# A constant's tile made 128 bytes wider in a three-stage Fourier and MoE kernel

## The chip, the cores and the metric

The kernel runs on one core of a Trainium2 chip. The metric is the device time of one launch in microseconds (us), from the inputs in HBM to the output in HBM. Lower is better.

## What is computed

Three layers follow each other on 6016 rows (2 sequences of 3008) of 256 numbers, all in float32:

```python
X = np.fft.rfft(x, axis=1)
Yr = Xr @ w_r - Xi @ w_i + b_r
Yi = Xr @ w_i + Xi @ w_r + b_i
Yr, Yi = soft_shrink(Yr, 0.01), soft_shrink(Yi, 0.01)
x = np.fft.irfft(Yr + 1j * Yi, n=3008, axis=1).reshape(6016, 256)
h = x @ w_in                                   # 256 -> 2048
x = (h * np.clip(h + 3.0, 0.0, 6.0) / 6.0) @ w_out
g = x @ w_gate                                 # 256 -> 1536
out = (g / (1 + np.exp(-g)) * (x @ w_val)) @ w_out2
```

(`soft_shrink` stands for two lines of the reference.) The weights come as float64 and are turned into pairs of float32 numbers in the kernel.

## The kernel before

**Stages.** The transform comes first, as small products with tables (`pre`, L275; `s2`, L336; `ln`, L356 to L375; `ia`, L382). `post` (L473) finishes the way back for one block of tokens. The first expert layer runs in units: 12 blocks of 512 or 448 tokens times 16 slices of 128 hidden columns. A unit is `project1` (six matmuls into `ph`, L117 to L119) and, two units later, `outp` (six into `acc`). The second expert layer runs in 72 quads: 6 pairs of token blocks times 12 hidden slices. A quad has seven products of three matmuls each (`product`, L716 to L718, into the banks `P`, `Tb`, `Q`) and, for the quad before it, four shares of three (`share`, again L117 to L119, into `acc`). Here the two token blocks of a pair enter through sums and differences that are held in seven tiles `xo`, the moving operands of the products.

**Three matmuls for a product.** Every operand of the expert layers and of `ln` is held as a high and a low part of type float32r, and each product is low times high, high times low, high times high (`mm3`, L116). In a matmul the first operand is the stationary one, which is loaded into the array ahead of it, and the second moves through. The other products (`pre`, `s2`, `ia`, `post`) take float32 operands, and the trace shows two matmul records for each.

**Order of work.** The schedule is manual: each engine runs its instructions in the order in which the program issues them, and the order is written out in `seq`, `unit` and `quad`. DMAs go out on SP's queue, a few on those of ACT and POOL. Nothing in the order depends on an address.

**Where tiles lie.** SBUF is filled from two ends. Pools of the side "left" are stacked from low addresses up, those of the side "right" from high addresses down. The left side begins with a scratch area of 8192 bytes and four constants of 32 bytes each; then come `misc` (L124), `wst` (L134), `rings` (L207) and later `cv` (L566). The right side holds `edge` (L136, 480 bytes that nothing uses), `w1`, for the transform `attn`, and from the second layer on `p2` (L696). The seven tiles `xo` of pair p are taken from the pool `xo[p % 2]` (L646): pairs 0, 2 and 4 from `cv` on the left, pairs 1, 3 and 5 from `p2` on the right (L624, L697). The addresses in the built program, in bytes within a partition:

| tiles | side | first byte | remainder by 512 |
|---|---|---|---|
| `fwd1_sb`, `inv2_sb`, `three` | left | 8320, 9088, 9472 | 128, 384, 256 |
| `zeros` and all tiles of `wst`, `rings` (`room0`, `room1`, `xa`, `r`, `ct`, `gh`, `gl`) | left | 9600 to 66944 | 384 |
| tiles of `cv`: `full`, `slot`, `raw`, `xo` of pairs 0, 2, 4, `T` | left | 68992 to 155008 | 384 |
| tiles of `attn` (`linh`, `linl`, `X`, `room2`, `room3`, `z`, `m`, `n`, `yp`) | right | 70144 to 161280 | 0 |
| `w1`, the weights of the first layer | right | 163328, 196096 | 0 |
| tiles of `p2`: `c`, `h`, `s`, `xo` of pairs 1, 3, 5 | right | 181760 to 224768 | 0 |

The 128-column slices of the weights that one matmul loads are 512 bytes long, and the rows of all operands in the expert layers are multiples of 512 bytes apart, so a slice has the remainder of its tile. In `ln` the slices of `X` have the remainders 0 and 256, and `linh`, `linl` 0.

Of the kernel before, what the change touches and what calls it, by code (L numbers as in the profile page):

```python
# [9 lines left out]
F32 = mybir.dt.float32  # L10
# [71 lines left out]
def fourier_moe_kernel(ctx: ExitStack, tc: tile.TileContext, x, lin, bias, w1, w2, fwd1, inv2, fwd2,  # L82
# [3 lines left out]
    def pool(stack, name, side):  # L86
        return stack.enter_context(tc.tile_pool(name=name, bufs=1, side=side))
# [36 lines left out]
    misc = pool(ctx, "misc", "left")  # L124
    fwd1_sb = misc.tile([128, 2 * GW], F32, name="fwd1_sb")
    inv2_sb = misc.tile([GW, QP], F32, name="inv2_sb")

    three = misc.tile([128, 32], F32, name="three")[:, :1]
    nc.vector.memset(three, 3.0)
    zeros = misc.tile([128, 512], F32, name="zeros")  # L130
    nc.vector.memset(zeros, 0.0)
# [731 lines left out]
```

## Time and profile before

| | us |
|---|---|
| median of 3 runs | 1259.88 (1257.68 to 1259.9) |
| the profiled execution's own time | 1258.6 |
| its span, first to last instruction | 1256.8 |
| TensorE (PE) busy | 1240.8 |
| VectorE (DVE) busy | 811.7 |
| ScalarE (ACT) busy | 679.9 |

The span is what the trace covers; the time of the execution is 1.8 us longer. PE's clock was granted at 0.998 of full speed on the mean. Matmuls are pipelined and the trace models their ends, so the busy time of PE says only that it hardly ever stood still; how fast it went is read from the starts of its matmuls or from the mean length of one.

### The profile page before, as it was taken

How to read it: one execution, taken by the hardware profiler on the slowest of the kernel's cores; microseconds unless marked ns; L12 is line 12 of the kernel's file. 1: busy time of each engine (PE TensorE's matmuls, PEld its weight loads, DVE VectorE, ACT ScalarE, POOL GpSimd, SP SyncE). 2: the span in 40 equal slices, each digit the busy share in tenths (PEclk: the TensorE clock that was granted, in tenths of full speed). 3: DMA queues.
4: the chain of work that ended last, by engine and by line, in shares of the span. 5: the costliest groups of instructions: out<-in, count | busy, mean ns of one | idle time of the engine just before them, and what ended most of it. 6: DMA issues, size and time to landing. Idle time of an engine off the chain costs nothing.

```text
span 1256.8 us, 15921 instructions
## 1 busy us (share of the span) xinstructions
PE 1240.8 (99%) x5914; PEld 1033.7 (82%) x5914; DVE 811.7 (65%) x1426; ACT 679.9 (54%) x1216; POOL 11.1 (1%) x19
## 2 busy tenths in 40 slices
PE   8899999999999999999999999999999999999998
PEld 3799887888888888888899888888888888888897
DVE  3577685666666666566556577676676666666665
ACT  3355554555555555555455566555656555555554
POOL 3000000000000000000000000000000000000000
PEclk9999999999999999999999999999999999999999
DMA  7886233023132122132032244544644644544551
GB/s 276 301 260 203 72 93 106 26 99 102 63 99 94 55 79 76 63 99 90 38 105 90 75 177 171 201 170 151 218 156 172 230 151 151 214 154 163 207 184 73
DMA packets 48781, 172.90 MB, mean 138 GB/s; under 512 B 4720, under 2 KB 18256, under 8 KB 37072
## 3 DMA queue, kind: packets, MB, share of 16 engines
q1 hardware_dynamic: 41600, 162.85, 37.6%
q10 hardware_dynamic: 6912, 8.39, 1.9%
q8 instruction: 46, 0.75, 0.2%
q0 software_dynamic: 192, 0.66, 0.1%
q14 instruction: 31, 0.25, 0.1%
HBM read 132.81 MB, written 39.06 MB: 137 GB/s over the span
## 4 chain that ended last, share of the span: by engine, by line
PE 97%; DMA 2%; DVE 1%; ACT 1%; issue 0%; SPq 0%; ACTq 0%; DVEq 0%
PE acc L118 12%; PE acc L119 12%; PE acc L117 12%; PE ph L117 7%; PE ph L119 7%; PE ph L118 7%; PE P L716 5%; PE P L718 5%; PE P L717 5%; PE Tb L718 3%; PE Tb L717 3%; PE Tb L716 3%; PE p L473 3%; PE p L117 2%; PE p L119 2%; PE p L118 2%
## 5 line engine op out<-in xcount | busy, mean ns | idle before, releaser
L488 DVE SCALAR_TENSOR_TENSOR r<-r,ph 128x512 f32<-128x512 f32 (+1 forms) x192 | 129.5, 675 | 91.1 <-ACT r L487 91.0
L487 ACT ACTIVATE r<-ph,three 128x512 f32<-128x512 f32 (+1 forms) x192 | 130.2, 678 | 103.7 <-PE ph L119 88.4
L122 DVE TENSOR_TENSOR gl<-r,gh 128x512 fp32r<-128x512 f32 (+1 forms) x192 | 130.0, 677 | 81.0 <-ACT gh L506 79.7
L506 ACT CAST gh<-r 128x512 fp32r<-128x512 f32 (+1 forms) x192 | 117.4, 611 | 83.9 <-DVE r L488 81.4
L117 PE MATMUL ph<-xa,w 128*128 128x512 f32 (+1 forms) x384 | 153.4, 400 | 0.0
L117 PE MATMUL acc<-gh,w 128*128 128x512 f32 (+1 forms) x384 | 149.8, 390 | 1.0 <-ACT gh L506 1.0
L118 PE MATMUL acc<-gl,w 128*128 128x512 f32 (+1 forms) x384 | 149.9, 390 | 0.3 <-DVE gl L122 0.2
L119 PE MATMUL ph<-xa,w 128*128 128x512 f32 (+1 forms) x384 | 149.8, 390 | 0.0
L118 PE MATMUL ph<-xa,w 128*128 128x512 f32 (+1 forms) x384 | 149.7, 390 | 0.0
L119 PE MATMUL acc<-gh,w 128*128 128x512 f32 (+1 forms) x384 | 149.7, 390 | 0.0
L122 DVE TENSOR_TENSOR gl<-s,gh 128x512 fp32r<-128x512 f32 (+1 forms) x144 | 97.2, 675 | 49.7 <-ACT gh L740 49.7
L716 PE MATMUL P<-xo,slot 128*128 128x512 f32 (+1 forms) x288 | 111.8, 388 | 1.7 <-DVE g L786 0.8
L118 PE MATMUL acc<-gl,slot 128*128 128x512 f32 (+1 forms) x288 | 111.9, 388 | 0.3 <-DVE gl L122 0.2
L718 PE MATMUL P<-xo,slot 128*128 128x512 f32 (+1 forms) x288 | 111.4, 387 | 0.0
L119 PE MATMUL acc<-gh,slot 128*128 128x512 f32 (+1 forms) x288 | 111.4, 387 | 0.0
L717 PE MATMUL P<-xo,slot 128*128 128x512 f32 (+1 forms) x288 | 111.4, 387 | 0.0
L117 PE MATMUL acc<-gh,slot 128*128 128x512 f32 (+1 forms) x288 | 111.1, 386 | 0.0
L782 ACT ACTIVATE s<-g 128x512 f32<-128x512 f32 (+1 forms) x72 | 44.9, 623 | 94.2 <-DVE g L780 94.2
L740 ACT CAST gh<-s 128x512 fp32r<-128x512 f32 (+1 forms) x144 | 88.2, 612 | 1.5 <-DVE s L799 1.2
L117 PEld LDWEIGHTS acc<-gh,w 128*128 128x128 f32 x384 | 72.3, 188 | 16.6 <-ACT gh L506 1.4
L118 PEld LDWEIGHTS acc<-gl,w 128*128 128x128 f32 x384 | 72.3, 188 | 16.1 <-DVE gl L122 1.0
L119 PEld LDWEIGHTS acc<-gh,w 128*128 128x128 f32 x384 | 72.3, 188 | 15.1
(102 smaller groups left out, 2263.3 us busy)
## 6 DMA issues: line engine op xcount, KB each, us to landing
slot<-Wd SPq DMA_DIRECT2D x72, 1152.0 KB, 5.1
st<-in_w SPq DMA_DIRECT2D x68, 256.0 KB, 3.6
Wd<-slot SPq DMA_DIRECT2D x12, 1152.0 KB, 4.7
z<-Bd SPq DMA_DIRECT2D x12, 512.0 KB, 5.6
Cd<-cs ACTq DMA_DIRECT2D x12, 512.0 KB, 3.6
Xd<-x SPq DMA_DIRECT2D x20, 256.0 KB, 2.1
raw<-Xd SPq DMA_DIRECT2D x5, 1024.0 KB, 7.6
out_t<-osb SPq DMA_DIRECT2D x20, 256.0 KB, 2.2
```

Of the source, the lines that this page charges most:

```text
L117: nc.tensor.matmul(o, wl, xh, start=start, stop=False)
L118: nc.tensor.matmul(o, wh, xl, start=False, stop=False)
L119: nc.tensor.matmul(o, wh, xh, start=False, stop=stop)
L122: nc.vector.tensor_tensor(out=o, in0=full, in1=hi.bitcast(F32), op=ALU.subtract)
L487: nc.scalar.activation(r[:, :n], p[:, :n], AF.Relu, bias=three)
L488: nc.vector.scalar_tensor_tensor(out=r[:, :n], in0=r[:, :n], scalar=6.0, in1=p[:, :n], op0=ALU.min, op1=ALU.mult)
L506: nc.scalar.copy(hi[:, :n], g[:, :n])
L716: nc.tensor.matmul(o, wl, x[:, 0, :n], start=start, stop=False, skip_group_check=not start)
L717: nc.tensor.matmul(o, wh, x[:, 1, :n], start=False, stop=False, skip_group_check=not start)
L718: nc.tensor.matmul(o, wh, x[:, 0, :n], start=False, stop=True, skip_group_check=not start)
L740: nc.scalar.copy(hi[:, :nb], t[:, :nb])
L782: nc.scalar.activation(s0[:, :n], h, AF.Silu)
```

## The change

`three` is a tile of 128 bytes of which one float is used. It becomes 256 bytes wide. No instruction is added, removed or moved.

```diff
@@ -125,7 +125,7 @@
     fwd1_sb = misc.tile([128, 2 * GW], F32, name="fwd1_sb")
     inv2_sb = misc.tile([GW, QP], F32, name="inv2_sb")
 
-    three = misc.tile([128, 32], F32, name="three")[:, :1]
+    three = misc.tile([128, 64], F32, name="three")[:, :1]
     nc.vector.memset(three, 3.0)
     zeros = misc.tile([128, 512], F32, name="zeros")
     nc.vector.memset(zeros, 0.0)
```

Every left tile behind `three` begins 128 bytes higher, so at a multiple of 512 bytes. `fwd1_sb`, `inv2_sb`, `three` itself and all tiles of the right side stay where they are.

## Rows read from the trace of the kernel before

**Rows 1.** The page: busy time of each engine, and the chain that ended last.
```profile
PE 1240.8 (99%) x5914; PEld 1033.7 (82%) x5914; DVE 811.7 (65%) x1426; ACT 679.9 (54%) x1216; POOL 11.1 (1%) x19
...
PE 97%; DMA 2%; DVE 1%; ACT 1%; issue 0%; SPq 0%; ACTq 0%; DVEq 0%
```

**Rows 2.** Groups by shape, whole span: count, busy us, mean ns of one.
```profile
L119 PE MATMUL ph<-xa,w 128*128 128x512 f32 x320 | 126.3, 395 | 0.0
...
L119 PE MATMUL acc<-gh,w 128*128 128x448 f32 x64 | 23.4, 366 | 0.0
...
L716 PE MATMUL P<-xo,slot 128*128 128x512 f32 x240 | 94.2, 392 | 1.5 <-DVE g L786 0.8 <-ACT x L496 0.8
```

**Rows 3.** Five windows of 60 us in pairs 0 to 4: PE busy, (x) matmuls.
```profile
730.00:790.00 60.00, 60.00 (x266) 1.00 0.45 159
810.00:870.00 60.00, 60.00 (x260) 1.00 0.51 182
900.00:960.00 60.00, 60.00 (x267) 1.00 0.54 195
1000.00:1060.00 60.00, 60.00 (x260) 1.00 0.44 159
1090.00:1150.00 60.00, 60.00 (x267) 1.00 0.48 172
```

**Rows 4.** Groups by shape, PE, window 730 to 790 us (pair 0).
```profile
L717 PE MATMUL P<-xo,slot 128*128 128x512 f32 x33 | 12.8, 389 | 0.0
...
L117 PE MATMUL acc<-gh,slot 128*128 128x512 f32 x32 | 12.4, 389 | 0.0
```

**Rows 5.** The same for the window 810 to 870 us (pair 1).
```profile
L718 PE MATMUL P<-xo,slot 128*128 128x512 f32 x32 | 12.6, 394 | 0.0
L117 PE MATMUL acc<-gh,slot 128*128 128x512 f32 x32 | 12.5, 391 | 0.0
...
L717 PE MATMUL Q<-xo,slot 128*128 128x512 f32 x8 | 3.2, 397 | 0.0
```

**Rows 6.** Timeline of PE in pair 0: start us, length us.
```profile
744.69 0.39 PE L717 MATMUL P<-xo,slot 128*128 128x512 f32 x1
...
746.96 0.39 PE L718 MATMUL P<-xo,slot 128*128 128x512 f32 x1
```

**Rows 7.** Timeline of PE in pair 1.
```profile
846.33 0.39 PE L717 MATMUL Tb<-xo,slot 128*128 128x512 f32 x1
...
848.88 0.39 PE L117 MATMUL acc<-gh,slot 128*128 128x512 f32 x1
```

**Rows 8.** Groups by shape, PE, window 426 to 462 us (first layer).
```profile
L118 PE MATMUL ph<-xa,w 128*128 128x512 f32 x27 | 10.7, 395 | 0.0
...
L118 PE MATMUL acc<-gl,w 128*128 128x512 f32 x26 | 10.3, 394 | 0.0
```

**Rows 9.** The tile `linh` (stage `ln`): lengths in ns min/median/max.
```profile
L119 PE MATMUL p<-linh,X x192: 279/283/288, 33.5 to 193.3; 128*128 128x256 f32 x192
```

**Rows 10.** Groups by shape, PE, window 1180 to 1240 us (pair 5).
```profile
L118 PE MATMUL acc<-gl,slot 128*128 128x448 f32 x36 | 13.2, 368 | 0.0
L716 PE MATMUL P<-xo,slot 128*128 128x448 f32 x36 | 13.2, 365 | 0.0
...
L117 PE MATMUL acc<-gh,slot 128*128 128x448 f32 x36 | 13.0, 362 | 0.0
```

**Rows 11.** Groups by shape, PE, windows 10 to 13.3, then 13.4 to 16.7 us.
```profile
L275 PE MATMUL p<-room,fwd_sb 128*96 128x512 f32 x9 | 4.0, 592 | 0.0
```

**Rows 12.** Groups by line, PE, whole span: `post`.
```profile
L473 PE MATMUL p<-inv_sb,ct 96*128 96x94 f32 (+14 forms) x300 | 35.6, 269 | 0.0
```

**Rows 13.** Windows over all engines: PE, PEld, DVE, ACT busy us.
```profile
430.00:460.00 30.00, 30.00 (x131) 24.33 (x130) 18.52 (x36) 15.94 (x27) 0.00 (x0) 1.00 0.33 104
820.00:850.00 30.00, 30.00 (x130) 24.23 (x130) 21.53 (x34) 17.01 (x30) 0.00 (x0) 1.00 0.44 158
```

**Rows 14.** What PE waited for: us in total, times, longest us.
```profile
PE p L275 <- DMA room<-in_x: 4.7, 1, 4.7
...
PE acc L117 <- ACT gh L506: 1.0, 1, 1.0
```

**Rows 15.** The tile `room`: time of its loads from issue to landing.
```profile
DMA to landing us min/median/max: 4.7/6.3/8.0
```

## The prediction

> **What bounds the kernel now.** I read the page first. PE is busy for 99% of the span, and the chain that ended last lies 97% on PE [rows 1]. So a change that touches no instruction can only matter through the rate of the matmuls or through the few waits of PE. I then split the matmuls by shape [rows 2], and compared stretches that do the same work.
>
> The second expert layer gives that comparison. Its pairs 0 to 4 run the same quads with the same engines beside them. Yet in 60 us PE starts 266 or 267 matmuls in pairs 0, 2 and 4, and 260 in pairs 1 and 3, all with the clock at 1.00 (2.4 GHz) and PE never idle [rows 3]. By shape, every one of the twelve groups of pair 0 has a mean of 389 ns [rows 4]; in pair 1 the groups lie between 391 and 397 [rows 5], 393.8 weighted by their counts. The ends are modelled, so I checked the starts: ten steps in pair 0 take 2.27 us, 227 ns each [rows 6]; eleven in pair 1 take 2.55 us, 232 ns each [rows 7]. A difference in mean length is a difference in spacing.
>
> What alternates with the pairs is the place of `xo`: left in 0, 2, 4, right in 1, 3, 5. The stationary `slot` and the moving `gh`, `gl` are on the left in all. With `slot` and `xo` both at remainder 384 the spacing is 227 ns; with `slot` at 384 and `xo` at 0 it is 232. The shares of pair 1, whose own operands both lie at 384, are slow too (391 for L117), so an unequal neighbour disturbs them: the weights of one matmul are loaded while another one streams.
>
> The first layer fits. Its weights are at 0, its moving `xa`, `gh`, `gl` at 384, and its groups have 394 or 395 ns [rows 8], as in the odd pairs. And `ln`, with 256 columns, has both operands on the right, at 0 or 256 against 0: its median is 283, and no matmul of the 192 in the row is longer than 288 [rows 9]. My reading: a float32r matmul goes at 389 ns (512 columns) where the stationary and moving operands begin at the same place modulo 256 bytes, and 5 to 6 ns slower where they are 128 bytes apart.
>
> **The change part by part.** It lifts the left side by 128 bytes: remainder 384 becomes 0, which is that of the right side. Under the reading all float32r matmuls then meet equal remainders.
>
> First layer, 512 columns: 6 groups of 320 = 1920 matmuls [rows 2]. In a stretch without `post` the six groups average 394.8 [rows 8], against 389: 5.8 ns x 1920 = 11.2 us.
>
> First layer, 448 columns: 6 x 64 = 384 matmuls at 366 [rows 2]. No row shows them at the fast spacing. I take the straight line between the two fast rows, 283 at 256 columns and 389 at 512 [rows 4, 9]: 0.414 ns a column, so 389 - 64 x 0.414 = 362.5. That gives 3.5 x 384 = 1.3 us.
>
> Pairs 1 and 3: 12 quads x (21 + 12) = 396 matmuls each, 792 at 393.8 against 389: 4.8 x 792 = 3.8 us.
>
> Pair 5, mostly 448 columns: 396 matmuls; its twelve groups lie between 362 and 370, 365.4 weighted, of which three stand here [rows 10]. 365.4 - 362.5 = 2.9, x 396 = 1.1 us.
>
> Pairs 0, 2 and 4 and `ln`: already equal, 0.
>
> Sum: 11.2 + 1.3 + 3.8 + 1.1 = 17.4 us.
>
> Against it stand the operands that do not move. `inv2_sb` stays at 384 while `ct` goes to 0, so `post` turns from equal to unequal; in `pre`, `fwd1_sb` stays while `room0` and `room1` move. These are float32. The `pre` row has 592 ns in the window of `room1` (384, weights at 0) and the identical 592 in that of `room2` (0, weights at 0) [rows 11]. I take 0, and as the far end 5.8 ns on each of the 300 matmuls of `post` [rows 12], 1.7 us.
>
> What hides the rest: PE faster by 2.4% asks the same of DVE and ACT. In a window of the first layer DVE is busy 18.5 of 30 us and ACT 15.9; in pair 1 21.5 and 17.0 [rows 13], and the fast pairs carry that second load at 227 ns without a wait. So I take 0 for new waits. If that cover were thinner than the shares say, the place would be `acc` L117 waiting for `gh`, 1.0 us in all today [rows 14]. The memory of `cv` reuses that of `attn`; as right tiles begin at remainder 0, the shift lets no `cv` tile reach into a further one, so no new wait for a release arises there.
>
> Transfers: their destination rows on the left begin 128 bytes higher. The trace of before cannot price this alone. Only one transfer costs PE much, `room`, 4.7 us in one wait [rows 14], with landings from 4.7 to 8.0 us [rows 15]. The ends are that this wait goes (-4.7) or that it grows by 8.0 - 4.7 = 3.3. I take 0, since the bytes and the order are the same, and the spread shows that such loads vary anyway.
>
> So 1258.6 - 17.4 = **1241.2 us**. This stands on the profiled execution's own 1258.6, which is 1.3 us below the median of the three runs; from the median the same sum gives 1242.5.
>
> **The rivals.** *It is the side, not the remainder.* Every fast case has both operands on one side, every slow one has one on each, so the rows fit as well if what matters is how far apart the operands lie. In pair 0 `slot` and `xo` are at most some 74 KB apart, in pair 1 at least 86 KB, in the first layer more than 94 KB. Then the change does nothing: 1258.6 to 1260. Against it: the left `xo` tiles of pair 0 reach from 122 to 151 KB while `slot` lies at 77 to 114, and all products have the same 389; a boundary would have to fall just between 151 and 163 KB, or a distance between 74 and 86.
>
> The Trainium skill, page "SBUF — State Buffer", section "Who interferes with whom", gives PE two independent read ports, one for the moving operand and one for weights, and says that PE never waits on anyone. By it the alignment would not matter at all, and the time would stay at the 1258.6 of the profiled execution. The trace does not agree with it as it stands: 389 against 393.8 ns, with nothing else changed than where `xo` lies.
>
> *Remainder 0 is the slow one.* With 512 columns, each slow stretch has one operand at 0, and the fast pairs have both at 384. If a stream or a weight load that begins at a multiple of 512 is the slow one, all would be slow after the change: the 3 x 396 = 1188 matmuls of pairs 0, 2 and 4 lose 5 to 6 ns each, some 6 us, and nothing is won: about 1264.6. What decides is whether `ln`, the one stage that has 0 against 0, is in the fast state. It speaks against this rival by its steadiness, 279 to 288 over 192 matmuls, where the slow groups of 512 mix shorter and longer ones.
>
> *Half is won.* Equal remainders may be needed but not enough: the spacing may lock only in some stretches, as the shares of pair 1 stay slow between unequal neighbours. With half of the sum won: 1258.6 - 8.7 = 1249.9.
>
> **How the numbers follow.** The forecast has 0.78, half won 0.07, the side 0.09, remainder 0 slow 0.06. The range holds the first two: its upper end is half won, 1250. Its lower end is the sum with part of the `room` wait gone as well, 1241.2 - 4.2 = 1237. The two others, 0.15, and the tails of the first two stay outside. About 0.2%, 2.5 us, is what a measurement of this kernel can tell from no change: faster 0.85, within that 0.09, slower 0.06.
>
> **What would show it.** In the changed kernel's profile, right: 266 or 267 matmuls in every 60 us of pairs 0 to 4; groups of 512 columns at 389 in the first layer and the odd pairs, and those of 448 near 362 or 363; pairs 0, 2, 4 and `ln` as they are. The side is right if the first layer still has 395 and pairs still alternate. Remainder 0 is the slow one if pairs 0, 2 and 4 go to 394 as well. The sum is wrong even with 389 everywhere if new waits of `acc` for `gh` or `gl`, or a longer wait for `room`, take part of it back.

## The result and the profile after

The changed kernel took 1244.89 us on the median of four runs (1241.29 to 1247.68), the kernel before beside it 1258.78: a ratio of 0.989, with a 95% interval of 0.9855 to 0.9925. So it is faster by 1.1%. The forecast was 1241.2 with a range of 1237 to 1250. The profiled execution of the changed kernel is the slowest of its four, 1247.68 us; its span is 1245.9 against 1256.8. The instruction counts of every engine are the same in both.

The page after, engines and chain, to be held against [rows 1]: PE still leads for 99% of the span, so the gain can only lie in how fast its matmuls follow each other.

```profile
PE 1228.6 (99%) x5914; PEld 1034.1 (83%) x5914; DVE 812.3 (65%) x1426; ACT 681.5 (55%) x1216; POOL 11.1 (1%) x19
...
PE 96%; DMA 2%; ACT 1%; DVE 1%; issue 0%; SPq 0%; ACTq 0%; DVEq 0%
```

The same five windows of 60 us as in [rows 3]; PE busy, the count of matmuls in brackets, then the granted clock. Pairs 1 and 3 (second and fourth line) had 260 and now have the 266 of the others:

```profile
730.00:790.00 60.00, 60.00 (x266) 1.00 0.44 158
810.00:870.00 60.00, 60.00 (x266) 1.00 0.49 172
900.00:960.00 60.00, 60.00 (x266) 1.00 0.48 170
1000.00:1060.00 60.00, 60.00 (x266) 1.00 0.44 158
1090.00:1150.00 60.00, 60.00 (x266) 1.00 0.44 158
```

Groups by shape of pair 1, window 810 to 870 us, and of the first layer, 430 to 454 us (mean ns of one behind the comma). The first answers to [rows 5], the second to [rows 8]; all twelve and all six groups now stand at the 389 of [rows 4], of which two each are shown:

```profile
L118 PE MATMUL acc<-gl,slot 128*128 128x512 f32 x33 | 12.8, 389 | 0.0
...
L716 PE MATMUL P<-xo,slot 128*128 128x512 f32 x32 | 12.4, 389 | 0.0
```

```profile
L118 PE MATMUL acc<-gl,w 128*128 128x512 f32 x18 | 7.0, 389 | 0.0
L119 PE MATMUL acc<-gh,w 128*128 128x512 f32 x18 | 7.0, 389 | 0.0
```

The 448-column matmuls did not follow. In the whole span those of the first layer, 366 in [rows 2], are at 367 to 370; pair 5, here between 1180 and 1230 us, stays at the 365 of [rows 10]:

```profile
L119 PE MATMUL acc<-gh,w 128*128 128x448 f32 x64 | 23.5, 367 | 0.0
L118 PE MATMUL ph<-xa,w 128*128 128x448 f32 x64 | 23.5, 367 | 0.0
```

```profile
L117 PE MATMUL acc<-gh,slot 128*128 128x448 f32 x32 | 11.7, 365 | 0.0
L119 PE MATMUL acc<-gh,slot 128*128 128x448 f32 x31 | 11.3, 365 | 0.0
```

What was to stay did: `ln` as in [rows 9], `post` as in [rows 12], although `ct` and `inv2_sb` now begin at different remainders.

```profile
L119 PE MATMUL p<-linh,X x192: 279/283/288, 34.5 to 196.4; 128*128 128x256 f32 x192
```

```profile
L473 PE MATMUL p<-inv_sb,ct 96*128 96x94 f32 (+14 forms) x300 | 35.6, 269 | 0.0
```

PE's waits, as in [rows 14]: that for `room` is 6.0 us here, that for `gh` 0.9 against 1.0, so DVE and ACT keep up.

```profile
PE p L275 <- DMA room<-in_x: 6.0, 1, 6.0
...
PE acc L117 <- ACT gh L506: 0.9, 1, 0.9
```

Three stretches account for the whole difference. The tile `ph` gives the marks: the first and the last start of its first matmul, before and after (lengths min/median/max, then first and last start in us).

```profile
L117 PE MATMUL ph<-xa,w x384: 358/392/583, 123.6 to 710.3; 128*128 128x512 f32 x160, 128*128 128x448 f32 x32
```

```profile
L117 PE MATMUL ph<-xa,w x384: 362/389/583, 127.2 to 704.2; 128*128 128x512 f32 x160, 128*128 128x448 f32 x32
```

| stretch | before | after | difference |
|---|---|---|---|
| start to the first `ph` | 123.6 | 127.2 | +3.6 |
| first to last `ph` (first layer) | 586.7 | 577.0 | -9.7 |
| last `ph` to the end (second layer) | 546.5 | 541.7 | -4.8 |
| span | 1256.8 | 1245.9 | -10.9 |

The 3.6 us at the start are the one part that lies elsewhere. The windows 50 to 75 us before, after, and in the run e3 below (PE, PEld, DVE, ACT, POOL busy, then the granted clock as a share, DMA share, GB/s) show a part of it:

```profile
50.00:75.00 25.00, 20.34 (x124) 16.29 (x123) 15.33 (x35) 10.24 (x26) 0.00 (x0) 0.93 0.88 289
```

```profile
50.00:75.00 25.00, 19.04 (x116) 16.16 (x115) 12.89 (x30) 9.34 (x23) 0.00 (x0) 0.86 0.75 247
```

```profile
50.00:75.00 25.00, 22.12 (x154) 19.26 (x154) 17.83 (x41) 12.46 (x31) 0.00 (x0) 1.00 0.84 274
```

PE waits for the last load of `room` here. Behind the wait the granted clock was at 0.50 (1.2 GHz) from 62 to 68 us in the changed kernel, at 0.57 on the mean from 60 to 64 us before, and at 1.00 (2.4 GHz) throughout in e3, whose longest wait was 2.9 us. The three kernels reach the first `ph` at 123.6, 127.2 and 121.0 us. The 3.6 us came in three parts of about the same size. Some 1.0 were there ahead of the wait: the last `pre` matmuls (L275) in front of it begin at 44.58 us before and at 45.53 after. The wait added 1.3 (6.0 against 4.7). Another 1.3 came behind it: from the end of the wait to the last `pre` matmul it took 14.0 us before, 15.3 after and 12.3 in e3, in the order of the clock. Over the ten profiles of this study that mark lies between 119.3 and 127.2 and shows no order by the place of the tiles, and the changed kernel's own four runs differ by 6.4 us at mean clocks of 0.997 to 1.000. e1 and e3 below, with equal places too, reach it at 123.8 and 121.0. That these 3.6 us belong to the run and not to the change is likely, but not shown.

### The profile page after: what moved, and what is told of

Its sections match the earlier page's. It is cut to its first block, busy times and chain, and to the rows that moved or that the text cites. A ratio compares the mean times of both kernels' runs of the same rounds, so it can differ in the third digit from the quotient of the medians.

```text
span 1245.9 us, 15921 instructions
## 1 busy us (share of the span) xinstructions
PE 1228.6 (99%) x5914; PEld 1034.1 (83%) x5914; DVE 812.3 (65%) x1426; ACT 681.5 (55%) x1216; POOL 11.1 (1%) x19
## 4 chain that ended last, share of the span: by engine, by line
PE 96%; DMA 2%; ACT 1%; DVE 1%; issue 0%; SPq 0%; ACTq 0%; DVEq 0%
PE acc L118 12%; PE acc L119 12%; PE acc L117 12%; PE ph L117 7%; PE ph L119 7%; PE ph L118 7%; PE P L716 5%; PE P L717 5%; PE P L718 5%; PE Tb L717 3%; PE Tb L716 3%; PE Tb L718 3%; PE p L473 3%; PE p L117 2%; PE p L336 2%; PE p L119 2%
## 5 line engine op out<-in xcount | busy, mean ns | idle before, releaser
L117 PE MATMUL acc<-gh,w 128*128 128x512 f32 (+1 forms) x384 | 148.3, 386 | 0.9 <-ACT gh L506 0.9
L119 PE MATMUL acc<-gh,w 128*128 128x512 f32 (+1 forms) x384 | 148.1, 386 | 0.0
L117 PEld LDWEIGHTS acc<-gh,w 128*128 128x128 f32 x384 | 72.1, 188 | 14.9 <-ACT gh L506 1.3
L119 PEld LDWEIGHTS ph<-xa,w 128*128 128x128 f32 x384 | 72.1, 188 | 13.9
```

The lines of the kernel that those rows point to most:

```text
L117: nc.tensor.matmul(o, wl, xh, start=start, stop=False)
L119: nc.tensor.matmul(o, wh, xh, start=False, stop=stop)
```

## The experiments

The theory of the prediction, called R below: a float32r matmul runs at its fast spacing where the stationary and the moving operand begin at the same place modulo 256 bytes. Eight kernels test it. Their two columns "first layer" (first to last `ph`) and "behind it" (last `ph` to the end) are taken from their rows as above, so that the start does not blur them. The place of a side is its remainder by 512. e5 to e8 ran once each, with one run of the kernel before beside them (1256.77 us); what is read from them rests on their traces, not on their times.

| kernel | left, right | time, us | ratio to before | first layer | behind it |
|---|---|---|---|---|---|
| before | 384, 0 | 1258.34 (13 runs) | | 586.7 | 546.5 |
| changed | 0, 0 | 1244.89 | 0.9890 (0.9855 to 0.9925) | 577.0 | 541.7 |
| e1 | 384, 384 | 1244.16 | 0.9884 (0.9861 to 0.9907) | 577.3 | 541.8 |
| e2 | 0, 384 | 1257.10 | 0.9987 (0.9974 to 1.0) | 586.6 | 546.4 |
| e3 | 256, 0 | 1244.65 | 0.9882 (0.9863 to 0.9901) | 577.5 | 541.8 |
| e5 | 64, 0 | 1246.49 (1 run) | | 579.0 | 546.4 |
| e6 | 32, 0 | 1257.67 (1 run) | | 588.5 | 546.6 |
| e8 | 192, 0 | 1257.33 (1 run) | | 587.2 | 545.0 |
| e7 | 0, 0, `cv` at 128 | 1253.74 (1 run) | | 577.1 | 551.7 |
| e4 | 0, 0, blocks 512 and 384 | 1243.65 | 0.9875 (0.9847 to 0.9902) | 576.0 | 541.2 |

### e1: both sides at 384

The kernel before, whose right side goes down instead:

```diff
-EDGE = 480
+EDGE = 608
```

> The kernel before with its right side lowered by 128 bytes, so that left and right both lie at remainder 384 and nothing at a multiple of 512. Theory R (what counts is that the stationary and the moving operand begin at equal remainders): the groups of 512 columns have 389 ns in the first layer and in all pairs, 266 matmuls in 60 us of pairs 1 and 3, time 1241 to 1248 us. Rival M (an operand must begin at a multiple of 512): first layer 395, odd pairs 394, perhaps pairs 0, 2, 4 as well, time 1256 us or more.

Its windows in pairs 0 and 1, and two groups of the first layer (430 to 454 us):

```profile
730.00:790.00 60.00, 60.00 (x267) 1.00 0.44 160
810.00:870.00 60.00, 60.00 (x267) 1.00 0.44 158
```

```profile
L119 PE MATMUL acc<-gh,w 128*128 128x512 f32 x18 | 7.0, 389 | 0.0
L117 PE MATMUL acc<-gh,w 128*128 128x512 f32 x18 | 7.0, 389 | 0.0
```

Nothing in the expert layers begins at a multiple of 512, and the whole gain is there. M falls. It is not the multiple of 512 that pays, but that the two agree.

### e2: left at 0, right at 384

The changed kernel with the same edit of `EDGE`.

> The changed kernel with its right side lowered by 128 bytes: left 0, right 384, so the two sides differ again. R: the kernel before comes back, 394 to 395 ns in the first layer and in pairs 1 and 3, 389 in pairs 0, 2 and 4, time 1256 to 1260 us. M: the left operands at multiples of 512 keep at least part of the gain, the first layer below 394 and the time below 1252 us.

```profile
730.00:790.00 60.00, 60.00 (x266) 1.00 0.44 159
810.00:870.00 60.00, 60.00 (x260) 1.00 0.50 176
```

```profile
L119 PE MATMUL ph<-xa,w 128*128 128x512 f32 x18 | 7.1, 395 | 0.0
L118 PE MATMUL ph<-xa,w 128*128 128x512 f32 x18 | 7.1, 394 | 0.0
```

The kernel before is back in both layers: 586.6 and 546.4 us against 586.7 and 546.5. That all left tiles lie at multiples of 512, as after the change, gains nothing when the right ones do not.

### e3: left at 256

```diff
-    three = misc.tile([128, 64], F32, name="three")[:, :1]
+    three = misc.tile([128, 128], F32, name="three")[:, :1]
```

> Left side at remainder 256, right side at 0: 256 bytes apart by 512, equal by 256. R by 256: 389 ns everywhere, time 1241 to 1248 us, as the changed kernel. R by 512: first layer and odd pairs slow, at 392 ns or more, time 1252 us or more.

```profile
730.00:790.00 60.00, 60.00 (x266) 1.00 0.44 158
810.00:870.00 60.00, 60.00 (x266) 1.00 0.44 159
```

Its first layer (430 to 454 us) stands at 389 too, in all six groups:

```profile
L119 PE MATMUL acc<-gh,w 128*128 128x512 f32 x18 | 7.0, 389 | 0.0
```

The period is 256 bytes, as `ln` had suggested [rows 9], not 512.

### e5, e6 and e8: left at 64, 32 and 192

The same line with `[128, 80]`, `[128, 72]` and `[128, 112]`.

> Left side at remainder 64, right side at 0. How far apart may the operands begin? Theory F (only exactly equal by 256 is fast): first layer and odd pairs at 392 ns or more, time 1252 us or more. Rival C (it is a coarse matter, 128 bytes or more apart): 389 ns everywhere, 1240 to 1248 us.

> Left side at remainder 32, right side at 0. F: first layer and odd pairs at 392 ns or more, time 1252 us or more. C: 389 ns everywhere, 1240 to 1248 us. If 64 is slow and 32 fast, the limit lies between them.

> Left side at remainder 192, right side at 0. If the distance counts around a circle of 256 bytes, 192 is 64 in the other direction, and the first layer and the odd pairs stand as with 64, up to a few ns if the sign matters.

First e5, three groups of the first layer (430 to 454 us) and two of pair 1 (810 to 870 us); then e6, the same with one group each; then e8:

```profile
L118 PE MATMUL acc<-gl,w 128*128 128x512 f32 x18 | 7.1, 394 | 0.0
L118 PE MATMUL ph<-xa,w 128*128 128x512 f32 x18 | 7.1, 394 | 0.0
...
L119 PE MATMUL ph<-xa,w 128*128 128x512 f32 x18 | 7.0, 388 | 0.0
```

```profile
L716 PE MATMUL P<-xo,slot 128*128 128x512 f32 x32 | 12.6, 394 | 0.0
L717 PE MATMUL P<-xo,slot 128*128 128x512 f32 x32 | 12.6, 394 | 0.0
```

```profile
L117 PE MATMUL acc<-gh,w 128*128 128x512 f32 x18 | 7.1, 395 | 0.0
```

```profile
L716 PE MATMUL P<-xo,slot 128*128 128x512 f32 x32 | 12.7, 396 | 0.0
```

```profile
L117 PE MATMUL ph<-xa,w 128*128 128x512 f32 x18 | 7.1, 394 | 0.0
```

```profile
L717 PE MATMUL P<-xo,slot 128*128 128x512 f32 x32 | 12.6, 392 | 0.0
```

C falls with e6: 32 bytes are enough for the full loss in the first layer and in the products, 395 and 396 ns. For 64 both theories miss in part. The products of e5's pair 1 have 394.3, which is against C. But its first layer has 391.3 weighted over its six groups, not the 392 or more of F, and keeps 7.7 of the 9.7 us (586.7 - 579.0), part of it in its 448-column blocks, while behind it nothing is left (546.4). The single time of e5, 1246.49, lies in the range of C and not in that of F; it flatters the kernel, as the first `ph` came at 119.3 us, 4.3 earlier than in the kernel before. In the first layer the moving operand lies on the left, in the products of the odd pairs on the right, so the same shift of the left side counts with opposite signs. With the signs taken in, e5 and e8 agree roughly: moving operand 64 further on, 391.3 (e5, first layer) and 393.0 (e8, products of pair 1); 64 back, 394.3 (e5, products) and 394.0 (e8, first layer). So the sign matters, as e8's text allowed, and 64 further on costs least of the unequal places that were tried.

### e7: only `cv` moved

The changed kernel with one line, behind which all lines of the second layer have a number one higher:

```diff
     cv = pool(ctx, "cv", "left")
+    cv.tile([128, 32], F32, name="shift")
```

> The changed kernel with an unused tile of 128 bytes ahead of slot, raw and the left xo: these lie at remainder 128, all else as in the changed kernel. First layer: equal, 389 ns. Pairs 0, 2, 4: slot and xo both at 128, gh and gl at 0, so the products are equal and the shares are not. Pairs 1, 3, 5: slot at 128 against 0 in products and shares. Theory O (each matmul pays for its own two operands): even pairs 389 for the products, 394 or more for the shares; odd pairs 394 in all. Rival N (the load of the next weights and the stream of the matmul in front meet, and the lag lasts for some matmuls): in the even pairs products and shares are mixed, 391 to 397, as in pair 1 of the kernel before; odd pairs 394 to 395 in all. Time under both about 1250 us: the phase of the second layer loses some 2376 x 5 ns = 12 us at most, the first layer keeps its 10.

Pair 0 in the window 730 to 790 us: three of the shares' groups and three of the products':

```profile
L119 PE MATMUL acc<-gh,slot 128*128 128x512 f32 x32 | 12.7, 396 | 0.0
...
L718 PE MATMUL P<-xo,slot 128*128 128x512 f32 x32 | 12.6, 394 | 0.0
L117 PE MATMUL acc<-gh,slot 128*128 128x512 f32 x32 | 12.6, 392 | 0.0
L118 PE MATMUL acc<-gl,slot 128*128 128x512 f32 x32 | 12.5, 392 | 0.0
...
L718 PE MATMUL Tb<-xo,slot 128*128 128x512 f32 x16 | 6.3, 396 | 0.0
...
L718 PE MATMUL Q<-xo,slot 128*128 128x512 f32 x8 | 3.1, 389 | 0.0
```

Products whose own operands are equal have up to 396, as N says and O does not: `Tb`, which follows a share, is slow, and `Q`, which comes nine matmuls with equal operands after the last share, is back at 389. The odd pairs have 394 or 395 in all groups. The first layer keeps its gain (577.1 us), and behind it the kernel is 5.2 us slower than before, because now pairs 0 to 4 are all disturbed. Against the changed kernel the second layer lost 10.0 of the 12 us put down as the most (551.7 against 541.7); the time was expected at about 1250 and came out at 1253.74. Each layer reacts to its own tiles alone.

### e4: 512 and 384 columns

```diff
-    blocks = [(a + (z - a) // 2 * i, a + (z - a) // 2 * (i + 1)) for a, z in pairs for i in range(2)]
+    blocks = [b for a, z in pairs for b in ((a, a + BLK), (a + BLK, z))]
```

> The changed kernel, whose last two token blocks of the first layer have 512 and 384 columns instead of 448 and 448. In the changed kernel the 448-column matmuls of the first layer stand at 368 ns, not at the 362.5 of a straight line between 256 and 512 columns. Theory L (a row of 448 floats is 1792 bytes, no multiple of 512, so that each matmul ends half a period off and the next weight load meets it unequal): 384 columns, 1536 bytes, lie on the line, 389 - 128 x 0.414 = 336 ns, and the blocks take 192 x (368 + 368 - 389 - 336) = 2.1 us less. Rival: shorter rows are slow by themselves, 384 columns then stand 5 ns or more above the line and nothing is won.

Two of the six groups of 384 columns, whole span:

```profile
L119 PE MATMUL acc<-gh,w 128*128 128x384 f32 x32 | 10.7, 335 | 0.0
L119 PE MATMUL ph<-xa,w 128*128 128x384 f32 x32 | 10.7, 335 | 0.0
```

384 columns lie on the line between 256 and 512 (335 against 336), 448 do not (367 to 370 against 362.5). The busy sums of the two blocks' groups are 1.6 us less (141.3 for 448 and 448; 75.3 + 64.4 for 512 and 384), where 2.1 were expected; by the starts the first layer is 1.0 shorter (576.0 against 577.0). What L said of the lengths came true. Its cause is not shown and does not go with e3: with a period of 256 bytes a row of 1792, which is 7 x 256, leaves no half period over. And with the left side at 64, 448 columns are fast too (e5, 360 to 363 in its first layer between 670 and 700 us), so the width alone does not make them slow. Why they are slow at equal places stays open. This kernel has the lowest median of all. But its interval contains the ratio of the changed kernel, and 1.6 us are within the scatter that the start brings; only the trace tells them apart.

## Why the prediction was right, point by point

**The mechanism held, and both rivals fell.** The step that carried the forecast, reading the alternation of the pairs as the place of `xo` against `slot`, was right. The rival of the side fell with the changed kernel itself: its weights and its moving operands are as far apart as before, and they run at 389. The rival of remainder 0 fell too: pairs 0, 2 and 4 stay at 389 with everything at 0. e1, e2 and e3 then tie it to equality modulo 256 from three sides.

**First layer, 512 columns**: forecast 11.2 us. The busy sums of the six groups fall from 761.4 to 751.9 us, 9.5; by the starts, which are measured where the lengths are modelled, the ten blocks are 10.2 us shorter. Nine of them gain 1.0 to 1.2 each, as forecast (5.8 ns x 192 = 1.1), the first one only 0.5. The term assumed 389 for all 1920. In the first block, which shares its stretch with the transform, units are broken up by other matmuls, and in the window 130 to 195 us the groups other than the first still have 389 to 392.

**First layer, 448 columns**: forecast 1.3 gained, measured 0.7 lost (busy sums 140.6 and 141.3), and 0.6 by the starts. This is the step that failed: "I take the straight line between the two fast rows". The line holds at 384 (e4), not at 448.

**Pairs 1 and 3**: forecast 3.8. Their mean went from 393.8 to 389, as said, but the modelled lengths show less than the starts. The first `Q` of pair 1 and that of pair 2, twelve quads later, before and after:

```profile
805.70 0.40 PE L716 MATMUL Q<-xo,slot 128*128 128x512 f32 x1
...
897.66 0.39 PE L716 MATMUL Q<-xo,slot 128*128 128x512 f32 x1
```

```profile
799.60 0.39 PE L716 MATMUL Q<-xo,slot 128*128 128x512 f32 x1
...
889.36 0.39 PE L716 MATMUL Q<-xo,slot 128*128 128x512 f32 x1
```

That is 91.96 us against 89.76, for 396 matmuls 232.2 ns each against 226.7, and pair 3 has the same: 4.4 us together. So this term was too small by 0.6, and the second layer as a whole fell by 4.8.

**Pair 5**: forecast 1.1, and nothing came: 365.2 before and 365.0 after in the window 1180 to 1230 us, weighted. The same straight line failed here. The forecast's 365.4 is moreover the mean of eleven groups, not twelve: the twelfth stands at 358, below the 362 to 370 that it names, and with it the mean is 365.1.

**What was put at nothing** held: `post` at 269 ns, float32 products untouched, no new wait of `acc`. Transfers had the ends -4.7 and +3.3, of which 0 was taken; the wait for `room` came out at +1.3, between them. With what lies ahead of the wait and behind it, for which the prediction had no term, the start is 3.6 longer in this profile.

**The sum**: forecast 17.4, measured 9.7 + 4.8 - 3.6 = 10.9 between the two profiles, and 13.9 between the medians. Without the start it is 14.5, so the sum was some 3 us too large, nearly all of it in the 448-column terms and the first block. The changed kernel's run at a mean clock of 1.000 took 1241.29, almost the forecast; that is luck, because the kernel before took 1255.44 in its own run at 1.000, 14.2 more and not 17.4. The rival "half is won" has no case of its own here: the 512-column matmuls won nearly all, the 448-column ones nothing.

**The rule of the skill.** The prediction set the Trainium skill's "SBUF — State Buffer", section "Who interferes with whom", by which PE never waits on anyone, against the 389 and 393.8 of the trace. e1 to e3 decide it for the trace: the same matmuls stand at 389 or at 394 to 395 ns with the relative place of their operands alone.

## What to carry to other kernels

Where a kernel is bound by back-to-back float32r matmuls of 512 columns that load new weights each time, lay the stationary and the moving tiles at equal addresses modulo 256 bytes; a pad of one small tile does it, and equality is what counts, not a round address. To find such a loss, compare the mean length of one matmul, or the count in a fixed window, between stretches that do the same work on other tiles. For other rows, measure: at equal places 256, 384 and 512 columns lie on one line here (283, 335 and 389 ns), and 448 columns, a row of 1792 bytes, lie above it and gained nothing.

## What the runs showed of the hardware that was not expected

Even 32 bytes apart cost the full 6 ns (395 against 389 in the first layer), while the moving operand 64 bytes further on costs some two fifths of that in the first layer (391.3) and more in the products of pair 1 (393.0), and 64 back nearly all (394).

A disturbed matmul passes its delay on: in e7 a product with equal operands right behind a share has up to 396 ns, and nine matmuls later 389 is reached again. How long it lasts is not the same everywhere: in pair 1 of e6 the first matmul of a share has 394 on the mean, and the next two, with equal operands like the first, are at 389.

In the first layer 448 columns behave the other way round: equal places gave 367 to 370, more than the 366 with 128 bytes between them, and with the moving operand 64 bytes further on they reach 360 to 363, around the straight line's 362.5. Pair 5 does not show this: 365.0 at equal places, 365.2 at 128 bytes. What inside the chip has a period of 256 bytes, and why the best place depends on the row's length, is left open.
